# Table products of the second assignment moved from GpSimd to VectorE, weight conversions held back, router work in portions of six

## The chip, the cores and the metric

One core of a Trainium2 chip runs the whole program. The metric is the device time of one execution in microseconds (us). The engines are TensorE (PE, with its weight load PEld), VectorE (DVE), ScalarE (ACT), GpSimd (POOL) and SyncE (SP), which here only issues DMAs. Each engine runs its own instructions strictly in the order in which they were written; between engines they wait by semaphores.

## The reference

Three stages, one after the other, on 4 x 576 = 2304 tokens:

```python
# 1. attention, 4 batches x 8 heads, 576 x 64
scores = scale * q @ k.T
scores = where(scores >= max(scores) - tau, scores, -1e9)
x = softmax(scores) @ v                       # tokens x 512
# 2. mixture of 8 experts, one of them for each token
logits = x @ w_gate + modality_bias[modality_id]
e = argmax(logits); g = softmax(logits)[e]
x = g * (relu(x @ w1[e]) @ w2[e])             # 512 -> 1024 -> 512
# 3. a dense layer
h = x @ w_in                                  # 512 -> 2048
out = (h * sigmoid(1.702 * h)) @ w_out        # 2048 -> 512
```

## The kernel before

The program goes through three stages that overlap at their borders. **Attention** (`Attention.run`, to about 310 us) takes pairs of heads. **The experts** (about 322 to 553 us) run in five slots of tokens that have one expert each, four of 512 tokens and one (slot 4) of 384. **The dense layer** (from 553 us) runs over all tokens in blocks of up to 512.

**A slot** is eight steps, f = 0 to 7 (`ffn.step`). A step has first the products of the first layer for 128 hidden features (`s1`, 12 matmuls on line 945), then `hh` (ACT, relu, rounded) and `hl` (DVE, the rest that rounding leaves), and then the second layer of two steps earlier (`s2`, 12 matmuls on line 967, 9 in slot 4). Weights come raw by DMA (`ra`, `rb`, lines 1175 and 1178) and are split by ACT into a high part (`ah`, `bh`) and by DVE into a low part (`al`, `bl`, line 1186). `bl` of a pair of steps is written in the later step of the pair, behind `hl`, and the second matmul of the next step's `s2` reads it.

**The next slot's tokens** are prepared in the steps f = 3 or 4 to 7: at the end of a step PE transposes a quarter of them into the one buffer `av` (line 929), ACT writes `xh` from it, DVE writes `xl` (line 932); only then is `av` free for the next quarter.

**The router** decides which token goes where. It runs twice (`assign`): assignment A after three batches, while attention still runs; assignment B after the fourth, in slot 0. B's steps on DVE are many small instructions and then tables with one row per chunk of tokens: `OL` (line 845: low digit equals column, 20 chunks x 128, in parts of 5, 5 and 10 chunks) and `R` (line 851: high digit equals column, 20 x 48). `values(0)` and `values(1)` (line 858) multiply `R` by the two digits of the token's number. 20 matmuls (line 864) sum the tables up, and four small instructions make the lists, among them `gB`, by which slot 2 gathers its rows.

All of this is a list of items, `att.side`. `att.sides(n)` takes up to n yields or calls off the list (a None ends the portion). In the slots it is called twice in a step: behind `hl`, before `s2` (`mid3`), with n = 9, and at the step's end with n = 12. At slot 1, f = 1, what is left until the lists exist is taken at once.

**The conversion of the dense layer's weights** (`conv`, a `Pipe` of 15 pieces: `wi` 0 to 10, `wo` 0 to 3) is fed in between. A piece is a DMA of 512 KB (`cv_raw`, line 1084), then an "upper" (one ACT and three DVE instructions, lines 1089 to 1092) and a "lower" (one ACT and four DVE, lines 1098 to 1105), each a step later. A piece is started in each odd f; in every fourth step a lower and an upper stand together. What is not done after slot 4 is drained before the dense layer begins. 17 more pieces are converted in the first blocks of the dense layer (`convert_some`).

The order of all instructions is that of the Python code (`manual_schedule`): nothing reorders them.

Of the kernel before, what the change touches and what calls it, by code (L numbers as in the profile page):

```python
# [36 lines left out]
HO = True  # L37
# [485 lines left out]
class Router:  # L523
# [168 lines left out]
    def assign(self, ph, gate):  # L692
        nc, wk = self.nc, self.wk[ph]
        first = ph == "A"
# [7 lines left out]
        f, excl, end, base = (T([128, NE], x) for x in ("f", "excl", "end", "base"))  # L702
# [151 lines left out]
            )  # L854

        def values(i):
            eng = nc.vector if i and first else nc.gpsimd
            eng.tensor_mul(R[:, :, i, :], R[:, :, 1, :], self.idp[:, i, 0:n].unsqueeze(2).broadcast_to([128, n, nh]))

        def sum_up(c0, c1):  # L860
# [129 lines left out]
def moe_kernel(ctx, tc, kq, v, tau, mid, w_gate, mod_bias, w1, w2, w_in, w_out, out):  # L990
    nc = tc.nc
# [10 lines left out]
    router = Router(ctx, tc, mid, mod_bias, x_dram, ident, ps)  # L1002
# [19 lines left out]
    def slot_of(s):  # L1022
        return ("A", s) if s < NA else ("B", s - NA)

    def gather_slot(s):
        ph, j = slot_of(s)
        rows[s], items = gather_items(router.idx["g" + ph], 4 * j, (B - 1) * S if s < NA else NT, SLOT_TILES[s])
        return items
# [15 lines left out]
    att = Attention(early, late_ctx, tc, kq, v, tau, w_gate, x_dram, router, ident, ps)  # L1044
# [24 lines left out]
    def open_resident():  # L1069
        late_ctx.close()  # L1070
        res = RP("res", 1)
        R["wi"] = [res.tile([128, NWI, 4, 128], F32R, name=n) for n in ("wi_h", "wi_l")]
        R["wo"] = [res.tile([128, NWO, 512], F32R, name=n) for n in ("wo_h", "wo_l")]
        R["cv"], R["raw"] = RP("cv", 3), RP("cv_raw", 2)

    ffn = Ffn(tc, ident, ps)
# [35 lines left out]
    def piece(kind, f, dst, at):  # L1112
        src = w_in32[:, :, f * 128:(f + 1) * 128, :] if kind == "i" else w_out32[:, f]
        return convert(src, lambda: [flat(d, at) for d in dst])
# [48 lines left out]
    def slot(e_idx, g_rows, raw_tile, w_tile, put):  # L1163

        ev = nc.sync.value_load(e_idx, min_val=0, max_val=NE - 1)
        W = {}
        gate = id_p.tile([128, 4], F32, name="gate")

        def gates():
            for t in range(len(g_rows)):  # L1170
                nc.gpsimd.tensor_copy(gate[:, t:t + 1], g_rows[t][:, DM:DM + 1])

        def load(g):
            ra = raw_tile("ra", "p (k f) -> p k f", dict(k=4))
            nc.sync.dma_start(
                ra, w1[bass.ds(ev, 1), :, g * 256:(g + 1) * 256].rearrange("a (kd p) f -> p (a kd) f", p=128))
            rb = raw_tile("rb", "p (g d) -> p g d", dict(g=2))
            nc.sync.dma_start(
                rb, w2[bass.ds(ev, 1), g * 256:(g + 1) * 256, :].rearrange("a (g p) d -> p (a g) d", p=128))
            W[g] = [ra, rb]  # L1180

        def split(g, i):
            raw = W[g][i]
            hi, lo = (w_tile("ab"[i] + x, ("p (k f) -> p k f", "p (g d) -> p g d")[i], (dict(k=4), dict(g=2))[i]) for x in "hl")
            nc.scalar.copy(hi, raw)
            nc.vector.tensor_sub(lo, raw, hi.bitcast(F32))
            W["ab"[i], g] = [hi, lo]

        def out(t, yps):
            y, write = put(t)  # L1190
            if t % 2:
                nc.vector.tensor_scalar_mul(y[:, 0:DM], yps, gate[:, t:t + 1])
            else:
                nc.scalar.activation(y[:, 0:DM], yps, ACTF.Identity, scale=gate[:, t:t + 1])
            if write:
                write(y)

        return dict(
            nf=8, act=relu, out=out, gates=gates, load=load, split=split,
            wa=lambda f: [w[:, :, (f % 2) * 128:(f % 2) * 128 + 128] for w in W["a", f // 2]],  # L1200
            wb=lambda f: [w[:, f % 2, :] for w in W["b", f // 2]],
        )
# [11 lines left out]
    def make_slot(s):  # L1214
        ph, j = slot_of(s)

        def first(t):
            def write(y):
                nc.sync.dma_start(y_first[(4 * j + t) * 128:(4 * j + t + 1) * 128, :], y[:, 0:DM])

            return y_p.tile([128, YW], F32, name="y"), write

        def rest(t):
            def write(y):
                scatter(y_rest, router.idx["cB"][:, 4 * j + t:4 * j + t + 1], y, "y", "each token has one row, written once")

            y = y_p.tile([128, YW], F32, name="y")
            nc.gpsimd.tensor_copy(
                y[:, DM:YW], router.idx["sB"][:, 4 * j + t:4 * j + t + 1].broadcast_to([128, YW - DM]))
            return y, write  # L1230

        blk = blocks[s] = slot(
            router.idx["e" + ph][0:1, j:j + 1], rows[s],
            lambda n, r, kw: raw_p.tile([128, 1024], F32, name=n).rearrange(r, **kw),
            lambda n, r, kw: w_p.tile([128, 1024], F32R, name=n).rearrange(r, **kw),
            first if s < NA else rest)
        return ffn.xprep(blk, x_p, rows[s], wide=(s == 0)) + [blk["gates"]]
# [42 lines left out]
    def make_last(i):  # L1280
        src, r0, nt = bt[i]
        w = src.shape[1]
        rws = []
        for t in range(nt):
            r = xg_p.tile([128, XW], F32, name="xg")
            nc.sync.dma_start(r[:, 0:w], src[r0 + t * 128:r0 + (t + 1) * 128, :])
            rws.append(r)
        if i < NA:
            return last_block(nt, router.idx["sA"][:, 4 * i:4 * i + 4]), rws, []
        ids = id_p.tile([128, 4], I32, name="ids")  # L1290

        def copy():
            for t in range(nt):
                nc.gpsimd.tensor_copy(ids[:, t:t + 1], rws[t][:, DM:DM + 1])

        return last_block(nt, ids), rws, [copy]
# [10 lines left out]
    conv, xq, gq = None, [], []  # L1307
    for s in range(NS):
        blk = blocks[s]
        for f in range(8):  # L1310
            ffn.step(blk, f, (lambda: blk["split"](0, 1)) if f == 1 and HO else None, mid3=lambda: att.sides(9))
            f0 = F0[min(s, 2)]
            if s + 1 < NS and f in (f0, f0 + 1):
                if f == f0:
                    while slot_of(s + 1)[0] == "B" and "gB" not in router.idx:
                        att.sides(30)
                    gq = gather_slot(s + 1)
                for g in gq[0:2]:
                    g()
                gq = gq[2:]  # L1320
                if f == f0 + 1:
                    xq = make_slot(s + 1)
            if s + 1 == NS and f == f0:
                last, rws, more = make_last(0)
                xq = ffn.xprep(last, x_p, rws) + more
            nxt = blocks.get(s + 1)
            g = f // 2
            if f % 2 == 0:
                if g + 1 < 4:
                    blk["split"](g + 1, 0)  # L1330
                elif nxt:
                    nxt["split"](0, 0)
            else:
                if f > 1 or not HO:
                    blk["split"](g, 1)
                if g + 2 < 4:
                    blk["load"](g + 2)
                elif nxt:
                    nxt["load"](g - 2)
            if conv is None:  # L1340
                if not att.tail(6):
                    open_resident()
                    wi, wo = R["wi"], R["wo"]
                    conv = Pipe(
                        [piece("i", i, wi, i) for i in range(NWI)] + [piece("o", i, wo, i) for i in range(NWO)])
            elif f % 2 == 1 or len(conv.live) > 1:
                conv.step(f % 2)
            for _ in range((XP0 if s == 0 else XP)[f]):
                if xq:
                    xq.pop(0)()  # L1350
            att.sides(12)
    conv.drain()
    convert_loads(2)

    for i in range(len(bt)):
        blk, nxt, xq = last, None, []
# [20 lines left out]
    with tc.For_i(lo, hi, 1) as i:  # L1377
# [19 lines left out]
        def put(t):  # L1397
# [3 lines left out]
        blk = slot(  # L1401
            pick["eB"][0:1, 0:1], g_rows,
            lambda n, r, kw: R["raw"].tile([128, 512, 2], I32, name="cv_raw").bitcast(F32).rearrange("p a b -> p (a b)").rearrange(r, **kw),
            w_tile, put)
# [9 lines left out]
        blk = last_block(4, pick["sB"])  # L1414
# [67 lines left out]
```

## Time and profile before

| | us |
|---|---|
| median of 3 runs | 981.56 |
| lowest and highest | 980.26, 983.67 |
| the profiled execution | 980.59 |
| its span in the trace | 978.8 |
| PE busy in it | 930.2 |

The trace is of the profiled execution. Its times count from the span's start; some 1.8 us of the execution lie around the span. A line number says which line of the kernel issued an instruction, and `out<-in` names what it writes and reads.

### The profile page before, as it was taken

To read this page: it belongs to the slowest core of one execution; us is meant where nothing else is said; L and a number is where in the kernel's file an instruction comes from. 1 tells how busy PE (TensorE), PEld (TensorE's weight loads), DVE (VectorE), ACT (ScalarE), POOL (GpSimd) and SP (SyncE) were. 2 spreads that over 40 slices of the span, in tenths; PEclk is the share of its full clock that TensorE was granted. 3 is DMA by queue.
4 is the path that set the end of the run, shared out by engine and by line. 5 is a ranking of instruction groups with operands and counts; after the bars stand their busy time and mean duration, and the time that the engine had idled before them with its cause. 6 is when DMAs were issued, how large, how long until landed. Compare 5 with 4: busy or idle time off the path is not lost. (4 is left out here: it accounts for less than half of the span.)

```text
span 978.8 us, 13986 instructions
## 1 busy us (share of the span) xinstructions
PE 930.2 (95%) x5009; PEld 750.0 (77%) x5009; DVE 556.3 (57%) x1194; ACT 448.8 (46%) x803; POOL 237.7 (24%) x322
## 2 busy tenths in 40 slices
PE   7899899999988969999999999999999999999994
PEld 6677777777765758878888888888888888888884
DVE  5888888888795497787766479961111111111110
ACT  4677677777775424444444434542222222222221
POOL 5935465576404422020302010010001000100100
PEclk7999999999999989999999999999999999999998
DMA  6766654655505434556555135330011000100100
GB/s 198 168 193 171 150 145 116 162 145 132 120 2 157 135 90 171 172 197 211 175 162 180 57 96 163 108 108 1 1 44 44 1 1 22 44 1 1 44 1 24
DMA packets 61307, 100.59 MB, mean 103 GB/s; under 512 B 9073, under 2 KB 32625, under 8 KB 61234
## 3 DMA queue, kind: packets, MB, share of 16 engines
q1 hardware_dynamic: 57394, 87.15, 31.1%
q0 software_dynamic: 3840, 12.50, 3.8%
q8 instruction: 42, 0.69, 0.3%
q14 instruction: 31, 0.25, 0.1%
HBM read 63.99 MB, written 17.23 MB: 83 GB/s over the span
## 5 line engine op out<-in xcount | busy, mean ns | idle before, releaser
L1161 DVE TENSOR_TENSOR hl<-sg,hh 128x512 fp32r<-128x512 f32 (+1 forms) x80 | 51.0, 638 | 242.9 <-ACT hh L1159 242.9
L1158 ACT ACTIVATE sg<-tr 128x512 f32<-128x512 f32 (+1 forms) x80 | 44.3, 554 | 208.4 <-PE tr L945 207.0
L245 DVE TENSOR_SCALAR_CACHE_REDUCE e<-sc,taue 128x576 f32<-128x576 f32 x144 | 116.3, 813 | 31.1 <-PE sc L234 27.3
L251 ACT ACTIVATE e<-e,thr 128x576 f32<-128x576 f32 x144 | 111.1, 776 | 31.3 <-DVE e L245 30.6
L234 PE MATMUL sc<-kA,qT 128*128 128x288 f32 x320 | 104.4, 342 | 20.7 <-DVE E L275 16.3
L945 PE MATMUL tr<-xh,wi_h 128*128 128x512 f32 (+1 forms) x320 | 120.6, 377 | 0.0
L945 PE MATMUL tr<-xh,wi_l 128*128 128x512 f32 (+1 forms) x320 | 118.8, 371 | 0.0
L945 PE MATMUL tr<-xl,wi_h 128*128 128x512 f32 (+1 forms) x320 | 118.7, 371 | 0.0
L967 PE MATMUL sc<-wo_h,hl 128*128 128x512 f32 x288 | 113.8, 395 | 0.0
L967 PE MATMUL sc<-wo_l,hh 128*128 128x512 f32 x288 | 113.7, 395 | 0.0
L967 PE MATMUL sc<-wo_h,hh 128*128 128x512 f32 x288 | 113.5, 394 | 0.0
L275 DVE SCALAR_TENSOR_TENSOR E<-sc,thr,e 128x576 f32<-128x576 f32 x128 | 103.4, 815 | 8.4 <-ACT e L251 5.0
L304 ACT COPY AT<-tr 128x512 f32<-128x512 f32 x128 | 73.9, 577 | 43.3 <-PE tr L302 43.2
L234 PE MATMUL sc<-kB,qT 128*128 128x288 f32 x320 | 91.2, 301 | 0.5 <-DVE kB L215 0.5
L234 PEld LDWEIGHTS sc<-kA,qT 128*128 128x128 f32 x320 | 61.7, 193 | 37.7 <-issue 21.9
L302 PE MATMUL tr<-ident,E 128*128 128x128 f32 x512 | 79.2, 278 | 0.0
L348 PE MATMUL av<-AT,V 128*64 128x288 f32 x512 | 76.7, 419 | 0.0
L945 PEld LDWEIGHTS tr<-xh,wi_l 128*128 128x128 f32 x320 | 60.2, 188 | 11.4
L945 PEld LDWEIGHTS tr<-xl,wi_h 128*128 128x128 f32 x320 | 60.3, 188 | 11.2
L945 PEld LDWEIGHTS tr<-xh,wi_h 128*128 128x128 f32 x320 | 60.2, 188 | 11.1
L302 PEld LDWEIGHTS tr<-ident,E 128*128 128x128 f32 x512 | 64.3, 144 | 0.6 <-DVE r L284 0.4
L967 PEld LDWEIGHTS sc<-wo_h,hl 128*128 128x128 f32 x288 | 54.0, 187 | 13.0
(215 smaller groups left out, 1754.2 us busy)
## 6 DMA issues: line engine op xcount, KB each, us to landing
ra<-in_moe_w_dram SPq DMA_DIRECT2D x20, 512.0 KB, 5.6
rb<-in_moe_w_dram SPq DMA_DIRECT2D x20, 512.0 KB, 3.8
F<-in_kq_dram SPq DMA_DIRECT2D x15, 640.0 KB, 5.3
cv_raw<-in_moe_w_in_dram SPq DMA_DIRECT2D x16, 512.0 KB, 5.0
cv_raw<-in_moe_w_out_dram SPq DMA_DIRECT2D x16, 512.0 KB, 3.6
V<-in_vp_dram SPq DMA_DIRECT2D x16, 320.0 KB, 4.9
kA<-kA SPq DMA_DIRECT2D x15, 320.0 KB, 3.4
kB<-kB SPq DMA_DIRECT2D x15, 320.0 KB, 3.5
```

The source lines that it names most:

```text
L234: nc.tensor.matmul(sc[:, hf, 0:288], l, d[kk][:, c0 + hf * 288:c0 + (hf + 1) * 288], start=(i == 0), stop=(i == len(ops) - 1),)
L245: nc.vector.tensor_scalar(e, d["sc", w][:, :, 0:288], self.taue[:, 0:1], 3.0e38, op0=ALU.add, op1=ALU.min, accum_out=thr)
L251: self.nc.scalar.activation(d["e", w], d["e", w], ACTF.Exp, bias=d["thr", w][:, 0:1], scale=-1.0)
L275: nc.vector.scalar_tensor_tensor(out=E.rearrange("p (a c) -> p a c", a=2), in0=d["sc", w][:, :, 0:288], scalar=d["thr", w][:, 0:1], in1=d[ ...
L302: nc.tensor.transpose(tp[:, kc * 128:(kc + 1) * 128], E[:, k0 + kc * 128:k0 + (kc + 1) * 128], self.ident)
L304: copies.append(lambda: nc.scalar.copy(AT[:, h, :, c * 128:(c + 1) * 128], tp.rearrange("p (k c) -> p k c", k=4)))
L348: nc.tensor.matmul(d["av"][h * 64:(h + 1) * 64, 0:288], d["V"][:, h, kc, :], d["AT"][:, h, kc, hf * 288:(hf + 1) * 288], start=False, stop ...
L945: nc.tensor.matmul(hps[:, 0:T], w[:, kd, :], blk[x][:, kd, :], start=(i == 0), stop=(i == 11))
L967: nc.tensor.matmul(y, h[:, cs], w, start=(f == 0 and i == 0), stop=(f == blk["nf"] - 1 and i == 2))
L1158: nc.scalar.activation(sg, hps, ACTF.Gelu_apprx_sigmoid)
L1161: return [upper, lambda: nc.vector.tensor_sub(hl, sg, hh.bitcast(F32))]
```

## The change

Three edits:

1. `values(1)` of assignment A was on VectorE already. Now both products of B are there too; only `values(0)` of A stays on GpSimd. In B each stands behind a part of `OL`.
2. The portions of the router's list in a step are 6 and 6 instead of 9 and 12.
3. The conversion pipe does not step until the lists of assignment B exist (`"gB" in router.idx`), which is at slot 1, f = 1. It used to start in slot 0.

```diff
         def values(i):
-            eng = nc.vector if i and first else nc.gpsimd
+            eng = nc.gpsimd if first and not i else nc.vector
             eng.tensor_mul(R[:, :, i, :], R[:, :, 1, :], self.idp[:, i, 0:n].unsqueeze(2).broadcast_to([128, n, nh]))
...
-            ffn.step(blk, f, (lambda: blk["split"](0, 1)) if f == 1 and HO else None, mid3=lambda: att.sides(9))
+            ffn.step(blk, f, (lambda: blk["split"](0, 1)) if f == 1 and HO else None, mid3=lambda: att.sides(6))
...
-            elif f % 2 == 1 or len(conv.live) > 1:
+            elif "gB" in router.idx and (f % 2 == 1 or len(conv.live) > 1):
                 conv.step(f % 2)
...
-            att.sides(12)
+            att.sides(6)
```

On DVE in slot 0 this stood in a row before, from the end of step f = 3 on (`hl` is that of f = 4; `plf` holds the digits, `g` is the gate of the tokens, `hl`, `al` and `xl` belong to the slot, `cv_e` and `cv_a` to the conversion):

```order
L841 CAST plf<-pl 128x40
L851 TENSOR_TENSOR R<-iota,plf 128x20x48
L845 TENSOR_TENSOR OL<-iota,plf 128x640 x2
L845 TENSOR_TENSOR OL<-iota,plf 128x1280
L664 TENSOR_REDUCE g<-L 128x5
L666 TENSOR_SCALAR g<-g 128x5
L668 RECIPROCAL g<-g 128x5
L1150 SCALAR_TENSOR_TENSOR hl<-tr,hh 128x512
L1186 TENSOR_TENSOR al<-ra,ah 128x1024
L1101 TENSOR_SCALAR cv_e<-cv_a 128x512
L1102 SCALAR_TENSOR_TENSOR cv_e<-cv_raw,cv_e 128x512
```

and this stands there now, from the end of step f = 4 on (`hl` is that of f = 5):

```order
L841 CAST plf<-pl 128x40
L851 TENSOR_TENSOR R<-iota,plf 128x20x48
L845 TENSOR_TENSOR OL<-iota,plf 128x640
L858 TENSOR_TENSOR R<-R,idp 128x20x48
L1150 SCALAR_TENSOR_TENSOR hl<-tr,hh 128x512
L845 TENSOR_TENSOR OL<-iota,plf 128x640
L858 TENSOR_TENSOR R<-R,idp 128x20x48
L845 TENSOR_TENSOR OL<-iota,plf 128x1280
L664 TENSOR_REDUCE g<-L 128x5
L666 TENSOR_SCALAR g<-g 128x5
L668 RECIPROCAL g<-g 128x5
L1186 TENSOR_TENSOR bl<-rb,bh 128x1024
```

The tables have the two products among them, they stand one step later, and no conversion follows: `bl` comes right behind the gate, where `hl`, `al` and conversions stood.

On POOL the products go, and nothing else changes (one piece of the difference):

```order
 L1011 DMA xg<-x_dram,igaA 128x528 x2
 L678 TENSOR_TENSOR pre<-pre,oh 128x8 x5
-L858 TENSOR_TENSOR R<-R,idp 128x20x48 x2
 L670 COPY g_4287<-g 128x80
 L1171 COPY gate<-xg 128x1 x4
```

The gate's copy, whose DMA the next weights on SP stand behind, now waits for nothing of POOL's own.

Three pieces that were converted in slot 0 push all others later, and the last of them into slot 4. On DVE there, in its step f = 4, this stood before:

```order
L1150 SCALAR_TENSOR_TENSOR hl<-tr,hh 128x384
L1186 TENSOR_TENSOR al<-ra,ah 128x1024
L932 SCALAR_TENSOR_TENSOR xl<-av,xh 128x512
L1150 SCALAR_TENSOR_TENSOR hl<-tr,hh 128x384
L1186 TENSOR_TENSOR bl<-rb,bh 128x1024
```

and now:

```order
L1150 SCALAR_TENSOR_TENSOR hl<-tr,hh 128x384
L1186 TENSOR_TENSOR al<-ra,ah 128x1024
L1101 TENSOR_SCALAR cv_e<-cv_a 128x512
L1102 SCALAR_TENSOR_TENSOR cv_e<-cv_raw,cv_e 128x512
L1104 TENSOR_TENSOR cv_a<-cv_a,wo_h 128x512
L1105 TENSOR_TENSOR wo_l<-cv_a,cv_e 128x512
L1090 TENSOR_SCALAR cv_a<-cv_a 128x512
L1091 TENSOR_SCALAR cv_a<-cv_a 128x512
L1092 SCALAR_TENSOR_TENSOR cv_a<-cv_raw,cv_a 128x512
L932 SCALAR_TENSOR_TENSOR xl<-av,xh 128x512
L1150 SCALAR_TENSOR_TENSOR hl<-tr,hh 128x384
L1186 TENSOR_TENSOR bl<-rb,bh 128x1024
```

Between `al` and `xl` of that step, where nothing was, seven instructions of the conversion now stand.

## Rows read from the trace of the kernel before

**Rows 1.** The page, part 1: busy time, share of the span, instructions, by engine

```profile
PE 930.2 (95%) x5009; PEld 750.0 (77%) x5009; DVE 556.3 (57%) x1194; ACT 448.8 (46%) x803; POOL 237.7 (24%) x322
```

**Rows 2.** Busy time by stretch: us, engines (count), granted clock, DMA share, GB/s

```profile
360.00:370.00 10.00, 6.64 (x25) 5.48 (x26) 8.64 (x15) 2.73 (x4) 0.00 (x0) 0.67 0.57 169
```

**Rows 3.** Waits of PE, 290 to 660 us: us in total, times, longest

```profile
PE av L929 <- DVE xl L932: 7.4, 1, 7.4
...
PE sc L967 <- DVE bl L1186: 0.5, 1, 0.5
```

**Rows 4.** PE in order of time: start us, us, instruction, [idle before it, releaser]

```profile
337.07 0.23 PE L712 MATMUL tr<-pre,ones 128*128 128x160 bf16 x1 [0.53 <-POOL pre L678]
...
343.02 0.60 PE L929 MATMUL av<-ident,xg 128*128 128x128 f32 x4
...
349.76 0.60 PE L929 MATMUL av<-ident,xg 128*128 128x128 f32 x4
...
351.60 0.40 PE L945 MATMUL tr<-xh,ah 128*128 128x512 f32 x1
...
355.54 0.39 PE L967 MATMUL sc<-bh,hl 128*128 128x512 f32 x1
363.36 1.11 PE L929 MATMUL av<-ident,xg 128*128 128x128 f32 x4 [7.43 <-DVE xl L932]
...
366.69 0.39 PE L945 MATMUL tr<-xh,ah 128*128 128x512 f32 x1
```

**Rows 5.** DVE in order of time, 343 to 363 us

```profile
343.74 0.16 DVE L772 TENSOR_SCALAR eiB<-ef 128x12 int32<-128x12 f32 x1
...
345.47 0.18 DVE L830 TENSOR_SCALAR pint<-pos 128x20 int32<-128x20 f32 x1
...
349.32 1.16 DVE L851 TENSOR_TENSOR R<-iota,plf 128x960 bf16<-128x960 f32 x1
350.40 6.16 DVE L845 TENSOR_TENSOR OL<-iota,plf 128x640 bf16<-128x640 f32 x3
...
357.00 0.65 DVE L1150 SCALAR_TENSOR_TENSOR hl<-tr,hh 128x512 fp32r<-128x512 f32 x1
357.57 1.22 DVE L1186 TENSOR_TENSOR al<-ra,ah 128x1024 fp32r<-128x1024 f32 x1
358.70 0.42 DVE L1101 TENSOR_SCALAR cv_e<-cv_a 128x512 int32<-128x512 int32 x1
...
361.09 0.42 DVE L1090 TENSOR_SCALAR cv_a<-cv_a 128x512 f32<-128x512 f32 x1
...
362.62 0.68 DVE L932 SCALAR_TENSOR_TENSOR xl<-av,xh 128x512 fp32r<-128x512 f32 x1
```

**Rows 6.** POOL in the same stretch

```profile
350.56 4.65 POOL L858 TENSOR_TENSOR R<-R,idp 128x960 bf16<-128x960 bf16 x2 [13.26 <-DVE R L851]
```

**Rows 7.** DVE in assignment A, 292 to 297 us

```profile
292.61 0.28 DVE L851 TENSOR_TENSOR R<-iota,plf 128x120 bf16<-128x120 f32 x1
292.81 0.82 DVE L845 TENSOR_TENSOR OL<-iota,plf 128x640 bf16<-128x640 f32 x1
...
296.03 0.28 DVE L858 TENSOR_TENSOR R<-R,idp 128x120 bf16<-128x120 bf16 x1 [0.48 <-POOL R L858]
```

**Rows 8.** ACT, the relu in the middle of slot 0

```profile
346.52 0.60 ACT L1149 ACTIVATE hh<-tr 128x512 fp32r<-128x512 f32 x1 [0.92 <-PE tr L945]
```

**Rows 9.** DVE in slot 4, the step with its fifth f

```profile
538.02 0.56 DVE L1150 SCALAR_TENSOR_TENSOR hl<-tr,hh 128x384 fp32r<-128x384 f32 x1 [2.02 <-ACT hh L1149]
538.96 1.22 DVE L1186 TENSOR_TENSOR al<-ra,ah 128x1024 fp32r<-128x1024 f32 x1 [0.38 <-ACT ah L1185]
```

**Rows 10.** PE in slot 4, the transposes at the next step's end

```profile
543.98 0.60 PE L929 MATMUL av<-ident,xg 128*128 128x128 f32 x4
```

**Rows 11.** SP, the first weights of slot 1 (issue)

```profile
358.92 0.46 SPq L1175 DMA_DIRECT2D ra<-in_moe_w_dram  x1
```

**Rows 12.** The page, part 6: DMA issues, KB each, median us from issue to landing

```profile
ra<-in_moe_w_dram SPq DMA_DIRECT2D x20, 512.0 KB, 5.6
```

## The prediction

> **What bounds the kernel now.** PE: it is busy for 930.2 of the 978.8 us of the span [rows 1], so only what stops PE counts. I read the stretches by time next. In the slots and the dense layer PE is full and its granted clock is 1.00, but for one place: from 360 to 370 us it is busy for 6.6 of 10 us at a mean granted clock of 0.67 [rows 2]: partly at the lower level of 1.2 GHz, partly at the full 2.4. The waits of PE name the cause: the one long wait from 290 us on is 7.4 us for `av`, until DVE has written `xl` (line 932); another is 0.5 us for `bl` [rows 3]. The order of time shows both ends of it. PE starts its last product at 355.54 and the next quarter's transposes at 363.36 [rows 4]. On DVE, `xl` of the quarter before starts at 362.62 and stands at the end of a row of work without a gap: `R` at 349.32, three parts of `OL` for 6.16 us, `hl`, `al`, and from 358.70 to 362.62 a lower and an upper of the conversion [rows 5]. So DVE, which on the whole is no bound, is one in slot 0: assignment B, the slot and the conversion come together there.
>
> What this costs in start times: 363.36 - 355.54 = 7.8 us against 0.23 from one product to the next, 7.6 lost. Then from the transposes at 363.36 to the seventh product behind them at 366.69 pass 3.33 us; the same seven at the full clock, from 349.76 to 351.60, take 1.84 [rows 4]. The clock had fallen to its lower level while PE stood still and took so long to come back: 1.5 lost. Together 9.1 us. The wait for `bl` makes one step 343.02 to 349.76 = 6.74 us long, where the next one took 355.54 + 0.23 - 349.76 = 6.0: 0.7 lost. And PE waits 0.53 us for the sums of `pre` by POOL [rows 4].
>
> **The change, part by part.** *Conversions held back.* Slot 0 loses on DVE a lower (358.70 to 361.09: 2.4 us) and an upper (361.09 to 362.62: 1.5) [rows 5] just ahead of `xl`, and as much around it. Their ACT instructions and the DMAs on SP ahead of the slot's weights go too; neither engine bounds there.
>
> *Portions of six.* The work is the same, in other places: sums of B now stand on PE behind the next `s1`, so POOL has 2.8 us more for `pre`, and the 0.5 us goes. `hl`, `al` and `bl` are no longer queued behind the whole of B, so the 0.7 goes as well. The tables move one step later, behind `xl`.
>
> *Products on DVE.* They add two instructions of 128 x 960 there. No row shows one of this size on DVE. The nearest are the comparison for `R`, of the same size, 349.32 to 350.40 = 1.08 us [rows 5], and the two on POOL, 4.65 us, 2.3 each [rows 6]. In assignment A product and comparison of 128 x 120 take the same 0.28 on DVE [rows 7], so I take 1.08 each. What goes in return: the three `OL` took 6.16 us [rows 5] while POOL ran its products from 350.56 for 4.65 us [rows 6]. Alone, a part of 5 chunks takes 0.82 [rows 7], of which some 0.08 overlap with the next; the 20 chunks would be 4 x 0.74 = 3.0. I take 3.0 and keep 6.2 for the range.
>
> The Trainium skill (VectorE: DVE Perf Modes, What auto-detection actually checks) has a double rate for two-input instructions whose tensors are all 16-bit with step 1 or -1. The product's tensors are 16-bit, but the digit is repeated with step 0; if that counted as a match, each product would take about 0.58 us (an estimate from the page), and the time would be 1.0 us lower. Rows 7 show no such rate at 128 x 120.
>
> *What is late next.* I follow DVE in its new order from `hl` of f = 4 to `bl` of the pair f = 4, 5, which stands right behind the gate: `hl` 0.57 (357.00 to 357.57), B's small ones up to `pint` 1.73 (343.74 to 345.47), `al` 1.13, `xl` 0.6, four small ones 0.6, `R` 1.08, `OL` 0.74, product 1.08, `hl` 0.57, `OL` 0.74, product 1.08, `OL` 1.48, the gate 0.44 (the tables' end at 356.56 to 357.00), `bl` 1.22 [rows 5, 7]: 13.1 us. It starts when ACT has written `hh`, 0.6 [rows 8], and a product's length of 0.4 [rows 4] plus a handover lie ahead of that: 1.1 after the start of the last product of f = 4. So `bl` is there 14.2 us after that start. PE wants it two steps and two products later: 2 x 6.0 + 0.46 = 12.5 [rows 4]. PE will wait 1.8 us for `bl`, in place of the 7.4 for `xl`; `xl`, next on DVE, is 0.6 behind `bl` and its reader 2.5, so it is in time. I charge no clock for 1.8 us: the clock fell during 7.4 us of standing still.
>
> *The same conversions later.* Three pieces of 2.4 + 1.5 = 3.9 us DVE each now fall into slot 4. DVE has room there, but one step is tight. In f = 4 a lower and an upper come between `al` and `xl`. `al` starts at 538.96 and leaves at 540.10, so `xl` runs 544.0 to 544.7, and PE wants `av` back at 543.98 [rows 9, 10]: 0.7 us wait. In the slots of 512 tokens the same pair has a step longer by 1.4 us to hide in, and costs nothing. If the hiding fails, it is 0.7 us in each of three more slots.
>
> *The lists.* Their 20 matmuls move behind the first `s1` of slot 1. Slot 2 wants its rows at slot 1, f = 4, three steps of 6 us behind: nothing.
>
> The sum: 9.1 + 0.7 + 0.5 - 1.8 - 0.7 = 7.8 us. The profiled execution, 980.59, becomes 972.8; it lies 0.97 below the median of 981.56, which becomes 973.8.
>
> **The rivals.** *DVE stays as slow at the tables* (`OL` slow by itself, not through POOL). Then the chain is 3.2 longer, PE waits 5.0 us, and the clock falls again, 1.5 more: 981.6 - 7.8 + 4.7 = 978.5. Against it is the 0.82 of A [rows 7]. The Trainium skill (SBUF — State Buffer, Who interferes with whom) says that a DVE instruction with two SBUF inputs contends with a GpSimd instruction that reads SBUF, and that the second waits for the whole of the first; by that rule the slow `OL` are POOL's doing and this rival falls, and rows 5 and 6, 6.16 us in the time of 4.65 us of POOL's, agree.
>
> *The weights of slot 1 come late.* On SP their first DMA stands behind the gate's, which now leaves DVE after the products. It was issued at 358.92, 1.9 us after the gate left DVE at 357.00 [rows 5, 11]. Now the gate is done 13.0 us after the last product of f = 4, at about 358.3; issue at 360.2, landing 5.6 later [rows 12], ACT's cast some 1.0: 366.8. PE wants it at about 368. That holds by 1.3 us; with a landing of 10 us PE waits 3: 976.8.
>
> *Slower: the conversions do not fit into slot 4.* Three pieces, 11.7 us of DVE, moved from where PE stood anyway into steps where it does not. If all of it ends on the path (each step of slot 4 waits for `bl` or `xl`, and the drain holds `hl` of the dense layer), 11.0 are added to the 0.7 counted: 984.8. It makes the whole slower from the point where more than 7.8 of the 11 stay uncovered. Against it: between `hl` at 538.02 and the transposes at 543.98 DVE does 0.5 + 1.1 + 0.6 of 6 us [rows 9, 10].
>
> *Nothing gained:* another wait of DVE on PE of the old size, in a place that I do not see: 980 to 982.
>
> **How the numbers follow.** Chances: forecast (971 to 977) 0.73, tables slow (977 to 980) 0.12, late weights (975 to 978) 0.06, slower 0.04, nothing gained 0.05. A measurement of this kernel can tell about 0.3%, 2.9 us, from no change. Faster than 978.6: 0.73 + 0.06 + half of the tables' case, some 0.86; within: 0.06 + 0.04, some 0.09; slower 0.05. The range goes from all waits gone (981.6 - 10.3 = 971.2) to 978.0, which takes in products as slow as POOL's (2.5 more wait, 976.3) and the late weights.
>
> **What would show it.** In the changed trace: no wait of PE for `xl` near 356 us and no fall of the clock in slot 0; a wait of 1 to 3 us for `bl` there; `OL` at 0.8 and 1.5, the products at 1.1 to 1.2 on DVE; a wait for `xl` below 1 us in slot 4, and PE full at the dense layer's start. I am wrong if the wait for `bl` is over 4 us, if the clock still falls in slot 0, or if slot 4 or the first steps of the dense layer show waits of several us.

## The result

The changed kernel takes 973.02 us (median of 4 runs, 972.62 to 973.11), the kernel before beside it 981.61 (980.26 to 983.67): a ratio of 0.9908, 95% interval 0.9893 to 0.9923. That is 0.9% faster, in the range and 0.8 us below the forecast. The profiled execution took 972.96 us with a span of 971.1, against 980.59 and 978.8 before: 7.6 us less, where the forecast for this execution was 7.8 (972.8).

PE stays the bound. The page of the changed kernel, part 1 (compare [rows 1]): PE does the same 5009 instructions in 1.6 us less busy time, and POOL has two instructions less, DVE two more.

```profile
PE 928.6 (96%) x5009; PEld 748.4 (77%) x5009; DVE 554.0 (57%) x1196; ACT 448.5 (46%) x803; POOL 230.9 (24%) x320
```

The waits of PE from 290 us on (us in total, times, longest) answer to [rows 3]: the 7.4 us for `xl` are gone, and three small waits stand there.

```profile
PE sc L967 <- DVE bl L1186: 1.6, 1, 1.6
...
PE av L929 <- DVE xl L932: 0.7, 1, 0.7
...
PE tr L945 <- DVE xl L932: 0.2, 1, 0.2
```

The stretches of the changed kernel (length, then busy us of PE, PEld, DVE, ACT, POOL; granted clock, DMA share, GB/s) answer to [rows 2]: from 360 to 370 us PE is full at clock 1.00, where it was busy for 6.64 at 0.67. The hole of the kernel before began at 355.9, so PE was busy for only 5.93 us of the stretch from 350 to 360 us too; now it is busy for 8.38 there, and 1.6 us is what is left of the hole.

```profile
350.00:360.00 10.00, 8.38 (x39) 6.53 (x38) 9.83 (x17) 2.72 (x4) 1.65 (x5) 1.00 0.00 0
360.00:370.00 10.00, 10.00 (x47) 8.10 (x47) 3.73 (x5) 2.97 (x4) 0.00 (x0) 1.00 0.52 161
```

PE in order of time, slot 0 and then slot 4 (start, us, instruction, [idle before it, releaser]; [rows 4, 10] are the same places before). The two steps of slot 0 from 341.76 to 353.78 are 6.01 us long each, then one product waits 1.62 for `bl`; in slot 4 the transposes wait 0.70 for `xl`, and the dense layer's first quarter waits 0.16. (The number in brackets counts from the end of the product before. Counted from start to start, as the prediction did, against 0.23 for products that follow each other, PE loses 359.03 - 357.02 - 0.23 = 1.78 us at `bl` and 535.72 - 534.62 - 0.23 = 0.87 at `xl`.)

```profile
341.76 0.60 PE L929 MATMUL av<-ident,xg 128*128 128x128 f32 x4
...
353.78 0.60 PE L929 MATMUL av<-ident,xg 128*128 128x128 f32 x4
...
359.03 0.50 PE L967 MATMUL sc<-bl,hh 128*128 128x512 f32 x1 [1.62 <-DVE bl L1186]
...
361.67 0.60 PE L929 MATMUL av<-ident,xg 128*128 128x128 f32 x4
...
489.57 0.49 PE L929 MATMUL av<-ident,xg 128*128 128x128 f32 x3
...
535.72 0.66 PE L929 MATMUL av<-ident,xg 128*128 128x128 f32 x4 [0.70 <-DVE xl L932]
...
548.06 0.51 PE L945 MATMUL tr<-xl,wi_h 128*128 128x512 f32 x1 [0.16 <-DVE xl L932]
...
589.01 0.60 PE L929 MATMUL av<-ident,xg 128*128 128x128 f32 x4
```

DVE in order of time in slot 0, the chain from `hl` to `bl` that the prediction followed (compare [rows 5 to 7]), and behind it slot 4, where a lower ends and an upper stands ahead of the late `xl`:

```profile
333.12 0.79 DVE L638 TENSOR_REDUCE L<-lgt 128x40 f32<-128x320 f32 x1 [0.88 <-POOL lgt L391]
...
345.89 0.69 DVE L1150 SCALAR_TENSOR_TENSOR hl<-tr,hh 128x512 fp32r<-128x512 f32 x1 [0.76 <-ACT hh L1149]
...
350.56 1.16 DVE L851 TENSOR_TENSOR R<-iota,plf 128x960 bf16<-128x960 f32 x1
351.64 0.82 DVE L845 TENSOR_TENSOR OL<-iota,plf 128x640 bf16<-128x640 f32 x1
352.37 1.15 DVE L858 TENSOR_TENSOR R<-R,idp 128x960 bf16<-128x960 bf16 x1
...
355.84 1.49 DVE L845 TENSOR_TENSOR OL<-iota,plf 128x1280 bf16<-128x1280 f32 x1
...
357.78 1.20 DVE L1186 TENSOR_TENSOR bl<-rb,bh 128x1024 fp32r<-128x1024 f32 x1
...
365.63 1.23 DVE L1186 TENSOR_TENSOR al<-ra,ah 128x1024 fp32r<-128x1024 f32 x1 [5.45 <-ACT ah L1185]
...
529.83 1.23 DVE L1186 TENSOR_TENSOR al<-ra,ah 128x1024 fp32r<-128x1024 f32 x1 [0.38 <-ACT ah L1185]
530.98 0.42 DVE L1101 TENSOR_SCALAR cv_e<-cv_a 128x512 int32<-128x512 int32 x1
...
534.37 0.69 DVE L1092 SCALAR_TENSOR_TENSOR cv_a<-cv_raw,cv_a 128x512 int32<-128x512 int32 x1
534.98 0.68 DVE L932 SCALAR_TENSOR_TENSOR xl<-av,xh 128x512 fp32r<-128x512 f32 x1
```

**Where the time went, along the program.** Three rows of the kernel before make it possible to compare places: the router's first row on DVE (L638), and transposes near the end of slot 3 and in the dense layer.

```profile
333.47 0.78 DVE L638 TENSOR_REDUCE L<-lgt 128x40 f32<-128x320 f32 x1 [0.88 <-POOL lgt L391]
...
498.71 0.49 PE L929 MATMUL av<-ident,xg 128*128 128x128 f32 x3
...
596.72 0.49 PE L929 MATMUL av<-ident,xg 128*128 128x128 f32 x3
```

No edit touches anything ahead of L638, and it starts 0.35 us earlier in the changed kernel (333.12). Measured from it, the transposes of 498.71 come at 489.57: 9.14 - 0.35 = 8.8 us are won through slots 0 to 3. Those of 543.98 in slot 4 [rows 10] come at 535.72, which leaves 7.9; those of 596.72 come at 589.01, which leaves 7.4. So slot 4 gives back 0.9, and the way from there into the dense layer 0.5.

### The profile page after: what moved, and what is told of

Its sections match the earlier page's. It is cut to its first block, busy times and chain, and to the rows that moved or that the text cites. A ratio compares the mean times of both kernels' runs of the same rounds, so it can differ in the third digit from the quotient of the medians.

```text
span 971.1 us, 13980 instructions
## 1 busy us (share of the span) xinstructions
PE 928.6 (96%) x5009; PEld 748.4 (77%) x5009; DVE 554.0 (57%) x1196; ACT 448.5 (46%) x803; POOL 230.9 (24%) x320
```

## The experiments

The last column is the time from L638 to the end of the profiled span, so that what varies ahead of the router (L638 starts between 332.9 and 335.5 us) drops out; it is that of one execution for each kernel. Ratios are to the kernel before on the same chip.

| kernel | median us | ratio, 95% interval | from L638 on, us |
|---|---|---|---|
| before | 981.61 | 1 | 645.3 |
| after | 973.02 | 0.9908 (0.9893 to 0.9923) | 638.0 |
| after_again | 973.52 | 0.9923 (0.9908 to 0.9938) | 637.9 |
| e_products | 980.02 | 0.9990 (0.9980 to 1.0000) | 644.7 |
| e_portions | 980.28 | 0.9992 (0.9982 to 1.0002) | 644.5 |
| e_held | 979.27 | 0.9976 (0.9966 to 0.9986) | 645.0 |
| u_products | 975.76 | 0.9943 (0.9924 to 0.9962) | 638.8 |
| u_portions | 978.32 | 0.9970 (0.9958 to 0.9981) | 642.3 |
| u_held | 979.57 | 0.9982 (0.9972 to 0.9991) | 644.4 |
| d_thrice | 977.88 | 0.9961 (0.9946 to 0.9975) | 642.4 |
| e_held_s1 | 976.00 | 0.9943 (0.9929 to 0.9957) | 641.4 |
| u_portions_s1 | 973.77 | 0.9927 (0.9912 to 0.9941) | 638.7 |
| b_both | 971.21 | 0.9897 (0.9880 to 0.9913) | 635.8 |
| b_gate | 972.77 | 0.9910 (0.9894 to 0.9925) | 636.7 |

### Each edit alone

Three kernels are the kernel before with one edit of the change: e_products with the first line below, e_portions with the second and third, e_held with the fourth.

```diff
-            eng = nc.vector if i and first else nc.gpsimd
+            eng = nc.gpsimd if first and not i else nc.vector
...
-            ffn.step(..., mid3=lambda: att.sides(9))
+            ffn.step(..., mid3=lambda: att.sides(6))
...
-            att.sides(12)
+            att.sides(6)
...
-            elif f % 2 == 1 or len(conv.live) > 1:
+            elif "gB" in router.idx and (f % 2 == 1 or len(conv.live) > 1):
```

> The first edit alone (both products of assignment B on VectorE, nothing else). Queue theory (TensorE stops because too much VectorE work of three kinds stands ahead of xl, and each edit takes its own share out): the tables and products take 3.0 + 2.2 = 5.2 us on VectorE in place of 6.2, so the wait for xl falls from 7.4 to about 6.4 us and the time from 981.6 to about 980.6. Rival (the contention of GpSimd's products with VectorE is the cause by itself): the wait falls by 3 us or more, 978 or below.

> The second edit alone (portions of six). Queue theory: the tables move one step later, behind one xl, but stand there among conversions and beside GpSimd's products; the wait moves from xl to bl: about 1 us for xl and 6 us for bl, with a fall of the clock; 980 to 981. Rival (the order of the router's work is the cause by itself): the wait goes, 973 to 975.

> The third edit alone (conversions held until the lists exist). Queue theory: 5.4 us of conversions go from ahead of the xl on which TensorE waits: the wait is about 2 us in place of 7.4, no fall of the clock; slot 4 has waits of 0.9 us as in the changed kernel; 975 to 976. Rival (the conversions are not the main part): above 978.

The first two came out as expected: next to nothing. In e_products the wait for `xl` is 6.4 in place of 7.4 us, and the clock still falls (360 to 370 us at 0.66). In e_portions the wait only changes its name; waits of PE, same columns as above:

```profile
PE sc L967 <- DVE bl L1186: 5.8, 1, 5.8
...
PE av L929 <- DVE xl L932: 1.4, 1, 1.4
```

DVE has the same row of work in front of it, and a different instruction of the slot stands at its end. The 3.9 us of a conversion that stand there keep the hole open whatever the other two edits do (u_held, below, has both of them and still waits 5.3).

e_held missed: 979.27 where 975 to 976 was expected. Its waits of PE:

```profile
PE tr L945 <- DVE xl L932: 3.2, 4, 1.1
...
PE av L929 <- DVE xl L932: 2.0, 1, 2.0
...
PE sc L967 <- DVE bl L1186: 1.5, 3, 0.7
```

The big wait shrank to 2.0 us, as it was meant to, but two things took its place. The clock fell behind this short wait too (rows in the last section), which makes the way from the transposes to the first product of the second layer 358.00 to 362.84 = 4.84 us, where the changed kernel takes 341.76 to 345.00 = 3.24: 1.6 lost. And slots 1 to 4 and the dense layer's first quarter show new waits for `xl` and `bl`, up to 1.1 us, which neither the kernel before nor the changed one has in that size. The traced execution, 980.46, is the slowest of nine; the fastest took 977.07, and whether the clock fell in that one no trace shows.

### Each edit undone

Three kernels are the changed one with one edit taken back (the diffs above, reversed).

> The changed kernel with conversions from slot 0 on again. Queue theory: about 4 us of conversions stand ahead of bl again: a wait of about 1 us for xl and of 5 us for bl, with a fall of the clock; slot 4 without waits; 979 to 980. Rival (conversions are not the main part): 973 to 975.

> The changed kernel with the products of assignment B back on GpSimd. Contention theory: the three parts of OL take about 6 us again in place of 3.1 on VectorE, while two products of 1.15 go from it: bl comes about 1 us later, the wait for it is about 2.5 us, time 973.8 to 974.3. Rival (no contention, OL is slow for its place): OL stays at 3.1, the wait for bl goes, 971.5.

> The changed kernel with portions of 9 and 12 again. Queue theory: the tables stand ahead of the older xl again, but alone: a wait for xl of about 1 us, the 0.7 us for the earlier bl and 0.5 us for the sums of GpSimd come back, the 1.6 us for the later bl goes; 974 to 975. Rival (the portions matter most): 978 or more.

u_held came out as expected in its time and in the main: waits of 2.0 for `xl` (about 1 was expected) and 5.3 for `bl`, the clock at 0.66 (362 to 364 us) and then 0.50 in the second, and 6.4 of the 7.3 us that the change wins from L638 on are gone. Holding the conversions back is what the other two edits rest on; by itself, in e_held, it brought little, for a reason that the runs below find.

u_products shows the contention. POOL and DVE of u_products in the same stretch:

```profile
353.14 4.64 POOL L858 TENSOR_TENSOR R<-R,idp 128x960 bf16<-128x960 bf16 x2 [14.30 <-DVE R L851]
```

```profile
352.98 0.82 DVE L845 TENSOR_TENSOR OL<-iota,plf 128x640 bf16<-128x640 f32 x1
...
354.32 4.82 DVE L845 TENSOR_TENSOR OL<-iota,plf 128x640 bf16<-128x640 f32 x2
```

The last two parts of `OL` take 4.82 us while POOL multiplies; in the changed kernel the same two take 0.82 and 1.49, some 2.2 when they follow each other. DVE loses 2.6 us to POOL's products, and making them itself costs it 2 x 1.07 = 2.1 (from one start to the next, 352.37 to 353.44 and 354.77 to 355.84). That is 0.5 for the edit, with 0.24 that DVE idles ahead of `bl`: PE waits 2.4 in place of 1.6 for `bl`. From L638 on the trace gives the same 0.8. Singly, the two parts took 1.82 and 3.08 us and ended at 356.14 and 359.14; POOL's products ended at 355.4 and 357.78. So each part ends 0.7 and 1.4 us behind a product, its undisturbed length, as if it had stood still for the whole of what was left of that product. The Trainium skill (SBUF — State Buffer, Who interferes with whom) says that a DVE instruction with two SBUF inputs contends with a GpSimd instruction that reads SBUF; these rows agree. The median, 975.76, lies above the 973.8 to 974.3 that was expected, and further from the 973.02 of the changed kernel than 0.8, each beside its own runs of the kernel before. The intervals of the ratios just miss each other, but that of the changed kernel made again (0.9908 to 0.9938) overlaps with it. The profiled u_products lost 1.3 us ahead of L638, where both are alike, and what the other runs lost there no trace shows; how much more than 0.8 the edit is worth here stays open.

u_portions missed: 978.32 where 974 to 975 was expected. Its waits in slot 0 were small, as expected, but the waits of e_held were back:

```profile
PE tr L945 <- DVE xl L932: 3.2, 4, 1.1
...
PE sc L967 <- DVE bl L1186: 1.6, 2, 1.3
PE av L929 <- DVE xl L932: 0.9, 1, 0.9
```

### Why larger portions cost time: the phase of the pipe

e_held and u_portions share one thing: with portions of nine and twelve the lists of B exist before slot 0 ends, so the held conversions start there (the first DMA of a piece is issued at 370.25 in u_portions, at 383.46 in the changed kernel). That is two steps off the place in which they start otherwise, half of the four steps in which their pattern repeats. At the border of slots 1 and 2 a lower, and no longer an upper, then stands ahead of the `xl` of slot 2's last quarter. DVE of u_portions there:

```profile
414.65 1.22 DVE L1186 TENSOR_TENSOR bl<-rb,bh 128x1024 fp32r<-128x1024 f32 x1
415.79 0.42 DVE L1101 TENSOR_SCALAR cv_e<-cv_a 128x512 int32<-128x512 int32 x1
...
417.57 0.69 DVE L1105 TENSOR_TENSOR wi_l<-cv_a,cv_e 128x512 fp32r<-128x512 f32 x1
418.18 0.68 DVE L932 SCALAR_TENSOR_TENSOR xl<-av,xh 128x512 fp32r<-128x512 f32 x1
```

and the same place in the changed kernel, with the shorter upper:

```profile
414.16 1.23 DVE L1186 TENSOR_TENSOR bl<-rb,bh 128x1024 fp32r<-128x1024 f32 x1
415.31 0.42 DVE L1090 TENSOR_SCALAR cv_a<-cv_a 128x512 f32<-128x512 f32 x1
...
416.83 0.68 DVE L932 SCALAR_TENSOR_TENSOR xl<-av,xh 128x512 fp32r<-128x512 f32 x1
```

A lower takes 418.18 - 415.79 = 2.4 us, an upper 1.5, so `xl` is 0.9 us later behind its `bl`. PE's product that reads it shows a wait of 0.57 at 418.92 in u_portions, 0.97 us behind the product before; in the changed kernel it shows none and starts 0.52 behind (0.23 would be its turn). To tell the phase from the portions themselves, two kernels hold the pipe until slot 1 as well: u_portions_s1 is u_portions, e_held_s1 is e_held, each with

```diff
-            elif "gB" in router.idx and (f % 2 == 1 or len(conv.live) > 1):
+            elif s and "gB" in router.idx and (f % 2 == 1 or len(conv.live) > 1):
```

> The changed kernel with portions of 9 and 12, and the conversion pipe held until slot 1 (and the lists). In the run with portions of 9 and 12 alone the lists exist in slot 0 already and the pipe starts there, two steps off its old place in the eight steps of a slot; in four places TensorE then waits for xl behind a lower (3.2 us) and once for bl (1.3 us). If that place in the slot is the cause, these go and the 0.9 us of the changed kernel's slot 4 come: 978.3 - 3.6 = 974.7. If the portions cost by themselves, 978.

> The kernel before with the conversion pipe held until slot 1 and nothing else. Same question for the third edit alone (979.3 measured, 975 to 976 had been expected): if the pipe's place in the slot is what took the gain, the waits for xl and bl in the later slots (4 us) go, 0.9 us in slot 4 come, and the time is about 976; otherwise it stays at 979.

Both came out as expected (u_portions_s1 0.9 us faster than named), and the repeated waits are gone. u_portions_s1 (973.77, 638.7 from L638 on) can't be told from the changed kernel made again beside it (973.52):

> The changed kernel once more, for comparison with the next on the same chip: 972.6 to 973.2.

So portions of six are worth 4.3 us (642.3 - 638.0) in this change only because they put the lists into slot 1, where the pipe then opens in its old phase. As portions they bring nothing that these runs can tell. e_held_s1 (976.0) gives conversions held back alone, in the right phase: 645.3 - 641.4 = 3.9 us from L638 on, more than half of what the change wins. Behind the changed kernel are 641.4 - 638.0 = 3.4 us, of which its wait of 2.0 in place of 1.6 and a clock that fell behind it (1.6, as in e_held) are the larger part. u_portions_s1 is e_held_s1 with the products on DVE: they win 641.4 - 638.7 = 2.7 us there (the medians of the same chip differ by 2.2), where alone, in e_products, they won 0.6. With them the wait falls to 0.9 and the clock stays up.

### How much room the products leave

d_thrice makes the first product of B three times (the same values), so DVE's chain to `bl` is two products longer:

```diff
-            eng.tensor_mul(R[:, :, i, :], ...)
+            for _ in range(1 if first or i else 3):
+                eng.tensor_mul(R[:, :, i, :], ...)
```

> The changed kernel with the first product of assignment B made three times on VectorE (same result). If VectorE's queue ahead of bl sets TensorE's wait one for one, 2.2 us are added to the wait of 1.6 us for bl: 3.8 us, and 975.2; if the granted clock falls in a wait of that length, 976 or more. Rival (something else is late there too, such as the raw weights of slot 1): less than 1 us is added.

PE waits 4.0 us in place of 1.6, all of the 2 x 1.19 = 2.4 that were added (three products take 3.54 us, one 1.15). And the clock falls, which costs 2.2 more: from the waiting product to the next transposes pass 363.43 to 368.29 = 4.86 us, where u_products, whose clock stayed up, takes 361.20 to 363.86 = 2.66. The sum, 4.6, is what the trace shows (642.4 - 638.0 = 4.4). The time, 977.88, is that of the expectation's case with a fall of the clock (976 or more). The chain to `bl` is on the path with its whole length: 2.4 us more of it cost 4.4, for the clock fell too.

### A version without the three waits

b_both is the changed kernel with two moves: `bl` is split ahead of the router's portion in a step, not behind it, and the quarter's `xl` is made ahead of the conversion's step.

```diff
+            def behind(blk=blk, f=f):
+                if f % 2 and f > 1:
+                    blk["split"](f // 2, 1)
+                att.sides(6)
+
-            ffn.step(..., mid3=lambda: att.sides(6))
+            ffn.step(..., mid3=behind)
...
-                if f > 1 or not HO:
-                    blk["split"](g, 1)
...
+            for _ in range((XP0 if s == 0 else XP)[f]):
+                if xq:
+                    xq.pop(0)()
             if conv is None:
...
-            for _ in range((XP0 if s == 0 else XP)[f]):
-                if xq:
-                    xq.pop(0)()
             att.sides(6)
```

> The changed kernel with two moves in writing order: bl of a pair ahead of the router's portion in its step (it is then ahead of half of the tables), and the next tokens' transposes with xh and xl ahead of the conversion in each step. If the two waits left (1.6 us for bl in slot 0; 0.7 and 0.2 us for xl in slot 4) are waits of TensorE on VectorE's queue, and nothing else is late behind them, both go: 973.0 - 2.5 = 970.5. If something else is late right behind (the raw weights of slot 1, or xl), 972 to 973.

It took 971.21 us. Its waits of PE in these stretches:

```profile
PE tr L945 <- DVE al L1186: 0.5, 1, 0.5
...
PE av L929 <- DVE xl L932: 0.2, 1, 0.2
```

The three waits are gone (638.0 to 635.8 from L638 on); 0.25 for `xl`, at 361.95 in slot 0, and 0.5 for `al` of slot 1 stand in their place. The 0.5 for `al` is the first of the late weights: the gate now leaves DVE behind `bl`, its DMA holds the first weights of slot 1 back on SP, and ACT's cast waits for them until 367.14. The intervals of the ratios overlap (0.9880 to 0.9913, and 0.9893 to 0.9923), so the medians alone do not settle that b_both is the faster one; the trace does, for its own execution.

b_gate takes b_both and makes B's gate right behind the ranks' matmuls, so that its DMA would be long gone from SP.

```diff
+        def early():
+            ranks()
+            if not first:
+                for _ in gate():
+                    pass
+
-            None, ranks, pages, ...
+            None, early, pages, ...
```

> The kernel with bl ahead of the router's portion and xl ahead of the conversion (971.2), and the gate of assignment B made right behind the matmuls of its ranks instead of behind the tables. There TensorE still waited 0.5 us for al of slot 1, whose raw weights are issued on SyncE behind the gate's DMA. If that DMA holds them back, the wait goes and the time is 970.5; if the weights are late for another reason, 971.2.

972.77 us: the expectation missed, and not better than b_both. The wait for `al` is gone, but 1.0 for `bl` and 1.0 for `xl` are back in slot 0. SP of b_gate shows why:

```profile
337.77 0.37 SPq L1184 DMA_DIRECT2D rb<-in_moe_w_dram  x1
346.45 1.58 SPq L674 DMA_DIRECT2D x_dram<-g  x2
348.25 0.55 SPq L1181 DMA_DIRECT2D ra<-in_moe_w_dram  x1
```

The gate's DMA waits there until 346.4, and slot 0's own weights, which in b_both were issued at 338.13, stand behind it until 348.25. ACT casts them at 352.48, and DVE idles 2.7 us for them in the step that has the tables. The queue keeps its order; an early gate only changes whose weights it holds back.

## The prediction, point by point

**The hole in slot 0.** Right: 7.6 of standing still and 1.5 of low clock went, and so did 0.7 for `bl` and 0.5 for POOL's sums. With the new wait, 9.1 + 0.7 + 0.5 - 1.8 = 8.5 were to be won up to slot 4; 8.8 were. What the 0.3 are the rows do not say.

**The chain to `bl`.** Right, term by term: from `hl` at 345.89 to the end of `bl` at 357.78 + 1.20 = 358.98 pass 13.1 us, as predicted. `OL` took 0.82, 0.82 and 1.49, the products 1.15 each, 1.07 from start to start, where 1.08 was taken. PE lost 1.78 us from start to start where 1.8 was predicted (the profile's 1.62 counts from the end of the product before), and the clock stayed at 1.00. The prediction charged no clock for this wait because it had fallen in one of 7.4; that was lucky in part, since in e_held and e_held_s1 the clock fell behind 2.0 us (last section).

**The double rate for the products.** It is not there: 128 x 960 with 16-bit inputs takes 1.15 us, as the comparison of the same size takes 1.16 with its f32 inputs. The estimate of 0.58 that the prediction took from the Trainium skill (VectorE: DVE Perf Modes, What auto-detection actually checks) needed the digit, repeated with step 0, to count as a match for the page's step of 1 or -1. It did not count: the trace agrees with the rule as it stands.

**Slot 4.** The 0.7 for `xl` came, by the mechanism named: seven instructions of the conversion between `al` and `xl`. From start to start, as it was worked out, it is 0.87, which is what slot 4 gives back. What was missed is a second place of the kind. At 545.79 an upper (1.5 us) stands ahead of the last `xl` of the dense layer's first quarter, and the product that needs it starts 0.55 us behind the one before (548.06 against 547.51), not 0.23; that is 0.3 of the 0.5 given back there. Together 7.4 are left of the 8.8, where 7.8 was forecast: 0.3 more won in slot 0 and 0.7 more given back behind it. The median fell by 8.6, more than the trace, because the traced execution of the kernel before was 1.0 us faster than its median; the 0.8 between forecast and median is no test of the sum.

**A slip.** The texts ahead say that three pieces move out of slot 0. Four start there before; the whole pipe is moved by four, and three of them start in slot 4 now. The cost in slot 4 was worked out from the order there, so the sum did not suffer.

**The rivals.** Tables slow by themselves: refuted, by 0.82 and 1.49 without POOL's products and 4.82 with them. Late weights: they were in time. The first weights were issued at 360.65, predicted 360.2, and landed in 3.9 us, not in the 5.6 of the median [rows 12]; `al` was written at 366.86. b_both, where the gate is later, shows the rival's first 0.5 us. Conversions that do not fit: not here, but e_held and u_portions show a form of it that the prediction did not have. They do fit in slots 1 to 4 in one phase, and cost waits of up to 1.1 in the other. The prediction took the phase for granted; it came right because of the portions.

**What each edit gives.** The prediction told the edits one by one but summed up the waits of the changed order as a whole, and so its sum did not need to know what each edit gives. What it did not say is that they do not add up. Alone they give 0.6, 0.8 and 0.3 us from L638 on (by the medians 1.2, 1.0 and 2.0); together 7.3. In the phase that the change has, the conversions give 3.9, the products then 2.7 and the portions the last 0.7, which the medians can't tell from nothing (973.77 and 973.52). The conversions and the products close the same hole, and the clock stays up only when little of it is left; the portions keep the phase.

## What to carry over

A stall of the bound engine behind a queue on another engine goes when all that stands in that queue's way goes; one cause taken out alone can show little (the products gave 0.6 us alone, and 2.7 once the conversions were gone), so price the queue from its start to the instruction that is waited for, and not edit by edit. When a periodic side job is delayed, look at its phase against the steps that it hides in, since half a period off a longer part of it may stand ahead of the instruction that is waited for. Moving a small DMA in an in-order queue changes which transfers wait behind it, so list what stands behind it in the new place, too.

## What was not expected of the hardware

**The clock falls behind short waits, but not behind all.** PE was full at clock 1.00 ahead of each of these waits. Behind 1.6 us (after) and 2.4 us (u_products) it stayed at 1.00. In e_held it fell after a wait of 2.0, and only when PE was at work again; the stretches of e_held around it, PE waiting in the first and starting again at 358.00:

```profile
356.00:358.00 2.00, 0.03 (x2) 0.01 (x1) 2.00 (x4) 0.00 (x0) 1.50 (x4) 1.00 0.12 15
358.00:360.00 2.00, 2.00 (x9) 1.65 (x10) 2.00 (x3) 0.58 (x1) 0.00 (x0) 0.71 0.66 131
360.00:362.00 2.00, 2.00 (x6) 1.56 (x5) 0.27 (x1) 0.00 (x0) 0.00 (x0) 0.50 0.94 197
362.00:364.00 2.00, 2.00 (x9) 1.61 (x8) 0.33 (x1) 0.96 (x2) 0.00 (x0) 0.94 0.95 321
```

and those of u_products, with the longer wait between 358.8 and 361.2 us:

```profile
358.00:360.00 2.00, 0.76 (x4) 0.28 (x2) 1.69 (x5) 0.60 (x1) 0.26 (x2) 1.00 0.00 0
360.00:362.00 2.00, 0.80 (x4) 0.67 (x4) 2.00 (x3) 0.00 (x0) 1.54 (x4) 1.00 0.12 15
362.00:364.00 2.00, 2.00 (x11) 1.60 (x10) 0.34 (x1) 0.00 (x0) 0.00 (x0) 1.00 0.65 123
```

e_held_s1 repeats the fall behind 2.0 us; u_held has the same 2.0 at a like place and no fall. The waits of 4.0 us and more (d_thrice, e_portions, e_products, u_held, before) all cost the clock, 1.5 to 2.2 us each. So among the waits of 1.6 to 2.4 us the length does not decide it by itself; no run has one between 2.4 and 4.0. The Trainium skill (TensorE: Matmul & The Clock Gate, What's actually happening) says that the activity is counted in windows that run on their own and do not start with the work; that the same wait falls differently into them would explain it. The traces do not show the windows, so this stays an explanation that was not shown.

**A small copy on POOL takes longer too.** The gate's copy of 128 x 80 on POOL took 1.16 us in the changed kernel, from 357.93, while DVE made `bl` (357.78 to 358.98). It took 1.16 in each of the five kernels in which it begins just behind the start of such a `bl`, and 0.25 in the others, u_products among them. `al` of slot 1, whose weights stand behind this copy's DMA, was in time all the same, so it costs nothing here.
